# Identity products on TensorE in the prelude of a chunked attention and SwiGLU kernel

## The chip, the cores and the metric

The kernel runs on one core of a Trainium2 chip. The metric is the device time of one execution in microseconds (us); lower is better. The engines are TensorE (PE, with its weight loads as PEld), VectorE (DVE), ScalarE (ACT), GpSimd (POOL) and SyncE (SP), which here only issues transfers.

## The reference

Attention inside chunks of 64 tokens, 8 heads of 64, 8 sequences of 576 tokens, and on its output, as 4608 rows of 512, an RMS norm and a gated feed-forward layer of width 1536:

```python
scores = scale * np.matmul(q_c, k_c.transpose(0, 1, 2, 4, 3))
scores = scores - np.max(scores, axis=-1, keepdims=True)
attn = np.exp(scores)
attn = attn / (np.sum(attn, axis=-1, keepdims=True) + 1e-09)
out = np.matmul(attn, v_c)
...
rms = np.sqrt(np.mean(x * x, axis=-1, keepdims=True) + 1e-06)
xn = x / rms * rms_g
g = xn @ w_gate
silu = g * (1.0 / (1.0 + np.exp(-g)))
val = xn @ w_val
return (silu * val @ w_out).astype(np.float32)
```

q, k, v are float32. The weights arrive as 64-bit numbers and are turned into float32 on the chip.

## The kernel before, in words

The 4608 rows go in nine tiles of 512. The first three ("plain" tiles, t = 0, 1, 2) are computed one by one: for each f of 12 blocks of the hidden width, `gated(f)` makes the gate (12 products of 128x512 into `ps_g`) and the value (12 into `ps_v`), Silu and their product `sg`, and `down(f - 1)` adds 12 products to four accumulators `acc`. The other six tiles go in three pairs through a scheme that saves products. Each operand is split in a high part `h` and a low part `l` of the type fp32r, and three products (h with h, l with h, h with l) stand for one. A product of the gate of f = 3 so needs both parts of its weights. `ps_g` and `ps_v` have one bank each: the gate of f + 1 waits for the Silu of f, the value of f + 1 for VectorE's product `sg` of f.

Attention works on units of 256 tokens, each two halves of 128 (i = 0, 1 are unit 0, i = 2, 3 unit 1). Per half: `scores` (products of 64x64), `softmax` on VectorE and the exponential on ScalarE (`e`), `att_transpose` (4 transposes into `ps_t`, copied by ScalarE to `eT`), `att_values` (into `ps_o`), `first_norm` (VectorE writes `x`). Then the squares are summed on ScalarE (`ss_u`), the root is taken on GpSimd (`ri_u`), ScalarE scales x, `x_turn_unit` transposes it on TensorE (`ps_x`), ScalarE makes `xh` and VectorE `xl`.

The prelude does this for units 0 and 1, and then tile 0 starts. Beside it, and through most of tile 0, the 18 blocks of weights are converted. Each takes a load (`raw`, 1 MB), two steps on ScalarE (the absolute value of the high word to `w`, and the low word scaled in place), three on VectorE (a clamp, a shift, the sign), a cast on ScalarE (high part of `parts`), and a subtraction on VectorE (low part). Blocks 0, 1, 3, 4, 6, 7 and so on hold the gate and value weights of f = 0, 1, 2, 3, 4, 5; the blocks between them hold output weights. Units 2 and 3 are worked on inside tile 0, at f = 0 and f = 5.

Until tile 1 the order of instructions on each engine is set by a scheduler from priorities (the order of the code, raised or lowered by `high_priority`) and its own estimates; each engine then works through its queue in that order. `tc.issue_after(x)` lets instructions of a block stand only behind x on x's engine. SyncE's queue is also in order: a store that waits for VectorE holds the loads behind it.

The prelude's main lines before:

```python
    scores(0, s0)
    scores(1, s1)
    softmax(0)
    softmax(1)
    att_transpose(0)
    softmax_sum(0)
    att_transpose(1)
    softmax_sum(1)
...
    scores(2, s2)
    scores(3, s2)
    softmax_both(1, s2)
```

Of the kernel before, what the change touches and what calls it, by code (L numbers as in the profile page):

```python
# [17 lines left out]
P = 128  # L18
# [62 lines left out]
def tile_chunk_attn_swiglu(  # L81
# [82 lines left out]

    conv = {}

    def conv_load(n):
# [4 lines left out]
    def conv_start(n):  # L172
        if n < len(pairs):
            words = raws[n].bitcast(I32).rearrange("p (n w) -> p n w", w=2)
            low, high = words[:, :, 0], words[:, :, 1]
            w = wp.tile([P, 2 * DM], F32, name="w")
            conv[n] = low, high, w
            nc.scalar.activation(w, high.bitcast(F32), AF.Abs, scale=2.0**16)  # L178
            nc.scalar.mul(low, low.bitcast(U32), LOW_SCALE)

    def conv_join(n):
        if n < len(pairs):


            low, high, w = conv[n]
            wi = w.bitcast(I32)
            nc.vector.tensor_scalar(w, w, HIGH_LEAST, HIGH_MOST, op0=ALU.max, op1=ALU.min)
            nc.vector.scalar_tensor_tensor(
                wi, wi, 3, low, op0=ALU.logical_shift_left, op1=ALU.bitwise_or
            )  # L190
            nc.vector.scalar_tensor_tensor(
                wi, high, -(2**31), wi, op0=ALU.bitwise_and, op1=ALU.bitwise_or
            )
# [10 lines left out]
            nc.scalar.copy(parts[:, 0].rearrange("p i c -> p (i c)"), w)  # L204
            if kind == "up":
                nc.sync.dma_start(wfd[f], w)

    def conv_end(n):
        if 0 <= n < len(pairs):
            w, parts = conv.pop(n)  # L210
            hi, lo = (parts[:, i].rearrange("p i c -> p (i c)") for i in range(2))
            nc.vector.tensor_tensor(lo, w, hi.bitcast(F32), op=ALU.subtract)

# [13 lines left out]

    state = {}

    def load_unit(u):  # L230
# [27 lines left out]
    def scores(i, banks):  # L258
        st, s = state[i], i % 2
        st["s"] = [b[:, s].rearrange("p (a k) -> p a k", k=CH) for b in banks]  # L260
        for pr in range(NPAIR):
            for j in range(2):
                for c in range(2):
                    tok = s * P + c * CH
                    rows = slice(j * D, (j + 1) * D)
                    nc.tensor.matmul(  # L266
                        st["s"][j][c * CH : (c + 1) * CH, pr],
                        st["q"][rows, pr, tok : tok + CH],
                        st["k"][rows, pr, tok : tok + CH],
                        start=True,  # L270
                        stop=True,
                    )

    def softmax(i):
# [8 lines left out]
        nc.scalar.activation(e, e, AF.Exp, scale=SCALE)  # L283

    def softmax_sum(i):
        st = state[i]
        rs = st["rs"] = small.tile([P, NPAIR, 2, 1], F32, name="rs")
        nc.vector.tensor_reduce(rs, st["e"], axis=AX.X, op=ALU.add)
        nc.vector.tensor_scalar_add(rs, rs, 1e-9)
        nc.vector.reciprocal(rs, rs)  # L290

# [26 lines left out]
    def att_transpose(i, pool=None):  # L318
        st = state[i]
        e = st["e"].rearrange("p a j k -> p a (j k)")  # L320
        eT = st["eT"] = att.tile([P, NPAIR, P], F32, tag="eT", name="eT")
        pt = bank(pool or ps_a, "ps_t").rearrange("p (a k) -> p a k", k=P)
        for pr in range(NPAIR):
            nc.tensor.transpose(pt[:, pr], e[:, pr], ident)
        nc.scalar.copy(eT, pt)

# [116 lines left out]
    def att_values(i, banks):  # L443
# [3 lines left out]
        for pr in range(NPAIR):  # L447
            for j in range(2):
                for c in range(2):
                    rows = slice(j * CH, (j + 1) * CH)  # L450
                    nc.tensor.matmul(
                        st["o"][j][c * CH : (c + 1) * CH, pr, :],
# [3 lines left out]
                        stop=True,  # L456
                    )

    def inv_rms(xs, spent):
# [45 lines left out]
    def x_turn_unit(u, d, pool):  # L505
        pt = state["xt", u, d] = bank(pool, "ps_x")
        for k in range(2):
            for s in range(2):
                at = (2 * k + s) * P
                src = x[:, 2 * u + s, (d + k) * P : (d + k + 1) * P]  # L510
                nc.tensor.transpose(pt[:, at : at + P], src, ident)

    def x_high_unit(u, d):
        pt = state["xt", u, d]
        for k in range(2):
            hi = xh[d + k][:, u * UT : (u + 1) * UT]
            nc.scalar.mul(hi, pt[:, k * UT : (k + 1) * UT], g_col[:, d + k : d + k + 1])  # L517

    def x_low_unit(u, d):
        pt = state.pop(("xt", u, d))  # L520
        for k in range(2):
            hi, lo = (part[d + k][:, u * UT : (u + 1) * UT] for part in (xh, xl))
            nc.vector.scalar_tensor_tensor(
                lo,
# [7 lines left out]
    def first_norm(i):  # L532
# [3 lines left out]
        for j in range(2):  # L536
            nc.vector.tensor_tensor(
                xv[:, j],
# [15 lines left out]
    def first_scale(u, shared):  # L554
# [5 lines left out]
        else:  # L560
            nc.scalar.mul(two, two, ri[:, 1:2])

    def softmax_both(u, banks):
# [5 lines left out]
        for j in range(2):  # L569
            by_row = banks[j].rearrange("p s (a k) -> p s a k", k=CH)  # L570
            nc.vector.tensor_reduce(mx[:, j], by_row, axis=AX.X, op=ALU.max)
            for s, (st, e) in enumerate(zip(both, es)):
                nc.vector.tensor_tensor(
                    e[:, :, j], st["s"][j], mx[:, j, s].broadcast_to([P, NPAIR, CH]), op=ALU.subtract
                )
        for e in es:
            nc.scalar.activation(e, e, AF.Exp, scale=SCALE)

# [538 lines left out]
    att_values(0, o)  # L1117
    first_norm(0)
    o = two_banks(ps_acc, "ps_o")
    att_values(1, o)  # L1120
    first_norm(1)
    scores(2, s2)
    scores(3, s2)
    softmax_both(1, s2)
# [6 lines left out]
    softmax_sum(3)  # L1131
    o = two_banks(ps_h, "ps_o")
    att_values(2, o)
# [190 lines left out]
```

## Time and profile before

| | us |
|---|---|
| median of 3 runs | 902.25 |
| lowest and highest | 901.88, 902.53 |
| profiled execution, its own time | 903.82 |
| its span (first to last instruction) | 902.0 |
| TensorE busy in it | 878.8 (97%) |
| mean granted TensorE clock | 0.99 |

How to read the rows. A row of the timeline gives the start in us from the span's start, the length, engine, line, operation, tiles (written <- read), shapes, how many instructions were put together (x32), and in brackets the idle time of the engine just before with what ended it. A row of the waits gives who waited for whom, then the total, how often and the longest. A row of the windows gives the stretch, and for PE, PEld, DVE, ACT and POOL the busy time and instructions, then the granted TensorE clock (1.00 is full), the share of the DMA engines and GB/s. Line numbers are those of the kernel before.

### The profile page before, as it was taken

Reading aid. Unit: us, or ns where it says so; the run is one execution under the profiler, and the core shown is the slowest. Engines: PE = TensorE matmul, PEld = TensorE weight load, DVE = VectorE, ACT = ScalarE, POOL = GpSimd, SP = SyncE. Lnnn points to the kernel's source line nnn. Section 1 sums busy time; section 2 is a strip of 40 time slices with the busy share of each in tenths; the row PEclk is TensorE's granted clock in tenths of the full one; section 3 lists DMA queues with packets and bytes.
Section 4 is the critical chain, followed back from the end, with each engine's and each line's share of the span. In section 5 each row is a group of like instructions: output and inputs, shape, how many; then the busy total and the mean of one; then the engine's idle time right before and its main releaser. Section 6 shows DMA issues by size and latency. Waiting matters only on the chain.

```text
span 902.0 us, 17424 instructions
## 1 busy us (share of the span) xinstructions
PE 878.8 (97%) x6828; PEld 720.7 (80%) x6828; DVE 606.3 (67%) x962; ACT 456.5 (51%) x775; POOL 181.3 (20%) x157
## 2 busy tenths in 40 slices
PE   4899999999999999999999999999999999999998
PEld 3688878888888888888888878888888888888886
DVE  6999865454568755985677987565769963334775
ACT  5997934343545564544545644336547432222452
POOL 0003040234200000233323002333330004323200
PEclk8799999999999999999999999999999999999999
DMA  9699999778977874887897867786866795445442
GB/s 350 271 340 325 323 329 360 244 235 258 301 247 242 236 222 148 317 272 263 269 322 286 303 249 282 244 297 212 303 231 245 277 342 187 156 157 199 180 163 94
DMA packets 85794, 231.84 MB, mean 257 GB/s; under 512 B 8912, under 2 KB 45264, under 8 KB 71504
## 3 DMA queue, kind: packets, MB, share of 16 engines
q1 hardware_dynamic: 84656, 230.20, 72.8%
q8 instruction: 54, 0.88, 0.4%
q10 hardware_dynamic: 1056, 0.52, 0.2%
q14 instruction: 28, 0.23, 0.1%
HBM read 167.25 MB, written 63.44 MB: 256 GB/s over the span
## 4 chain that ended last, share of the span: by engine, by line
PE 85%; ACT 6%; DMA 4%; DVE 3%; issue 1%; SPq 0%; POOL 0%; ACTq 0%; POOLq 0%
PE ps_c L820 11%; PE ps_a L820 11%; PE ps_b L820 11%; PE acc L627 9%; PE ps_g L592 8%; PE ps_v L592 8%; PE ps_d L820 6%; PE ps_c L1032 5%; PE ps_a L1032 5%; PE ps_b L1032 4%; PE ps_d L1032 3%; DMA wr<-wsd 2%; PE ps_o L393 2%; PE ps_s L266 2%; ACT w L178 1%; DMA raw<-w_up_dram 1%
## 5 line engine op out<-in xcount | busy, mean ns | idle before, releaser
L820 PE MATMUL ps_a<-xp,wr 128*128 128x512 f32 x432 | 104.5, 390 | 0.8 <-DMA wr<-wsd 0.7
L820 PE MATMUL ps_c<-xp,wr 128*128 128x512 f32 x432 | 104.6, 391 | 0.5 <-DMA wr<-wsd 0.5
L820 PE MATMUL ps_b<-xp,wr 128*128 128x512 f32 x432 | 104.5, 391 | 0.0
L592 PE MATMUL ps_g<-xh,parts 128*128 128x512 f32 x288 | 96.7, 396 | 0.9 <-ACT xh L517 0.6
L820 PEld LDWEIGHTS ps_a<-xp,wr 128*128 128x128 f32 x432 | 80.9, 188 | 18.5 <-DMA wr<-wsd 1.7
L592 PE MATMUL ps_v<-xh,parts 128*128 128x512 f32 x288 | 95.0, 390 | 0.5 <-DVE sg L614 0.5
L820 PEld LDWEIGHTS ps_c<-xp,wr 128*128 128x128 f32 x432 | 80.6, 188 | 17.6 <-issue 0.6
L820 PEld LDWEIGHTS ps_b<-xp,wr 128*128 128x128 f32 x432 | 80.7, 188 | 17.1
L627 PE MATMUL acc<-parts,gh 128*128 128x512 f32 x288 | 89.9, 394 | 0.0
L908 POOL TENSOR_TENSOR g<-u,u 128x512 f32<-128x512 f32 x18 | 23.2, 1288 | 269.7 <-ACT u L876 161.2
L592 PEld LDWEIGHTS ps_g<-xh,parts 128*128 128x128 f32 x288 | 54.4, 189 | 13.6 <-ACT sg L610 1.0
L592 PEld LDWEIGHTS ps_v<-xh,parts 128*128 128x128 f32 x288 | 54.2, 188 | 12.1 <-DVE sg L614 0.9
L940 ACT CAST gh<-g 128x512 fp32r<-128x512 f32 x72 | 43.6, 622 | 37.3 <-PE ps_b L1032 13.2
L627 PEld LDWEIGHTS acc<-parts,gh 128*128 128x128 f32 x288 | 53.2, 188 | 11.2
L945 DVE TENSOR_TENSOR gl<-g,gh 128x512 fp32r<-128x512 f32 x72 | 50.3, 705 | 15.8 <-PE ps_a L1032 6.6
L898 POOL TENSOR_TENSOR p<-p,p 128x512 f32<-128x512 f32 x36 | 46.7, 1308 | 53.0 <-DVE rs L354 35.9
L592 PE MATMUL ps_g<-xl,parts 128*128 128x512 f32 x144 | 56.5, 392 | 0.0
L627 PE MATMUL acc<-parts,gl 128*128 128x512 f32 x144 | 56.2, 390 | 0.0
L592 PE MATMUL ps_v<-xl,parts 128*128 128x512 f32 x144 | 56.0, 389 | 0.0
L876 ACT ACTIVATE p<-p 128x512 f32<-128x512 f32 x36 | 22.8, 633 | 58.4 <-POOL p L898 52.6
L820 PE MATMUL ps_d<-xp,wr 128*128 128x512 f32 x216 | 52.3, 391 | 0.0
L885 DVE TENSOR_TENSOR u<-ps_b,p 128x512 f32<-128x512 f32 x36 | 24.5, 687 | 40.1 <-PE ps_b L820 36.5
(150 smaller groups left out, 1701.5 us busy)
## 6 DMA issues: line engine op xcount, KB each, us to landing
wr<-wsd SPq DMA_DIRECT2D x63, 1024.0 KB, 6.8
wo<-osd SPq DMA_DIRECT2D x30, 1024.0 KB, 7.8
raw<-w_up_dram SPq DMA_DIRECT2D x12, 1024.0 KB, 10.6
vt<-v_dram SPq DMA_DIRECT2D x18, 512.0 KB, 6.1
wsd<-parts SPq DMA_DIRECT2D x18, 512.0 KB, 8.3
qt<-qT_dram SPq DMA_DIRECT2D x17, 512.0 KB, 5.2
kt<-kT_dram SPq DMA_DIRECT2D x17, 512.0 KB, 5.9
away_e<-e SPq DMA_DIRECT2D x28, 256.0 KB, 3.1
```

Of the source, the lines that this page charges most:

```text
L266: nc.tensor.matmul(st["s"][j][c * CH : (c + 1) * CH, pr], st["q"][rows, pr, tok : tok + CH], st["k"][rows, pr, tok : tok + CH], start=True ...
L393: nc.tensor.matmul(st["o"][(2 * c + t) * Q : (2 * c + t + 1) * Q, h * D : (h + 1) * D], eT[c][rows, t, h], vt[rows, c, h], start=True, sto ...
L592: nc.tensor.matmul(ps, a[f][:, cols], b[dt], start=(dt == 0 and i == 0), stop=(dt == NDT - 1 and i == 2),)
L627: nc.tensor.matmul(acc[s], a[:, cols], b, start=(f == 0 and i == 0), stop=(f == NF - 1 and i == 2),)
L820: nc.tensor.matmul(ps, w[:, a, m, cols], xp[:, b, kt], start=start and kt == 0 and i == 0, stop=stop and kt == 1 and i == 2, skip_group_ch ...
L876: nc.scalar.activation(t, t if src is None else src, AF.Silu)
L885: nc.vector.tensor_tensor(kp["u2"], b["b"], kp["p1"], op=add)
L898: nc.gpsimd.tensor_tensor(kp["p5"], kp["p1"], kp["p5"], op=add)
L908: nc.gpsimd.tensor_tensor(g[:, 0, 1], kp["u2"], kept[0]["u2"], op=mult)
L940: nc.scalar.copy(gh, src)
L945: nc.vector.tensor_tensor(gl, src, pair[0].bitcast(F32), op=ALU.subtract)
L1032: nc.tensor.matmul(banks[m][name], w[:, (0, 1, 0)[k], m * P : (m + 1) * P], (gh, gh, gl)[k], start=opens and i == 0 and k == 0, stop=not ( ...
```

## The change

A helper `keep_busy` is added, which multiplies the first columns of the 128x128 identity by themselves into a bank of PSUM that is not read afterwards, at low priority and behind a given instruction. `whole` products have 128 columns, `half` ones 64. It is called five times in the prelude: 2 + 14 products ahead of the first scores, 1 behind the transposes of half 0, 1 behind those of half 1, 6 + 20 behind the scores of half 3, and 10 + 10 behind the x transposes of unit 0: 64 products. Some steps are tied behind others with `issue_after`, and a table `CONV_BEHIND` of 25 entries ties steps of the first seven weight conversions on ScalarE and VectorE behind named steps of the prelude (the diff shows its first lines). The tile `ps_o` of half 2 is opened earlier in the code. No operation is removed.

```diff
+    CONV_BEHIND = {
+        (0, "abs"): ("exp", 1),
+        (0, "low"): ("eT", 1),
...
+    def behind(n, what):
+
+        held = ExitStack()
+        if (n, what) in CONV_BEHIND:
+            held.enter_context(tc.issue_after(mark[CONV_BEHIND[n, what]].ins))
+        return held
...
-            nc.scalar.activation(w, high.bitcast(F32), AF.Abs, scale=2.0**16)
-            nc.scalar.mul(low, low.bitcast(U32), LOW_SCALE)
+            with behind(n, "abs"):
+                nc.scalar.activation(w, high.bitcast(F32), AF.Abs, scale=2.0**16)
+            with behind(n, "low"):
+                nc.scalar.mul(low, low.bitcast(U32), LOW_SCALE)
...
+    def keep_busy(bank, whole, half, behind):
+
+        with ExitStack() as held:
+            held.enter_context(tc.high_priority(offset=-URGENT))
+            if behind is not None:
+                held.enter_context(tc.issue_after(behind.ins))
+            for cols in [P] * whole + [CH] * half:
+                one = ident[:, :cols]
+                done = nc.tensor.matmul(bank[:cols, 0, :cols], one, one, start=True, stop=True)
+        return done
...
-    scores(0, s0)
-    scores(1, s1)
+    with tc.issue_after(keep_busy(s2[0], 2, 14, None).ins):
+        done = scores(0, s0)
+    with tc.issue_after(done.ins):
+        done = scores(1, s1)
     softmax(0)
     softmax(1)
-    att_transpose(0)
+    with tc.issue_after(done.ins):
+        done = att_transpose(0)
+    keep_busy(s2[0], 1, 0, done)
     softmax_sum(0)
-    att_transpose(1)
-    softmax_sum(1)
+    with tc.issue_after(keep_busy(s2[0], 1, 0, att_transpose(1)).ins):
+        softmax_sum(1)
+        o = two_banks(ps_h, "ps_o")
+        att_values(0, o)
+        first_norm(0)
+        spare = o = two_banks(ps_acc, "ps_o")
+        done = att_values(1, o)
+        first_norm(1)
+    with tc.issue_after(done.ins):
+        scores(2, s2)
     o = two_banks(ps_h, "ps_o")
...
-    scores(3, s2)
+    asked = scores(3, s2)
...
     for d in range(0, NDT, 2):
-        x_turn_unit(0, d, ps_a)
+        first_turned = x_turn_unit(0, d, ps_a)
...
+    keep_busy(spare[0], 6, 20, asked)
+    keep_busy(spare[0], 10, 10, first_turned)
     conv_start(0)
     conv_step(EARLY)
```

What this does to the order shows at four places. In the rows a name is a tile (`ps_x` the x transposes, `xh_119` and `xl_123` the high and low part of x's first quarter), and line numbers after are those of the kernel after.

TensorE, end of the prelude, before:

```order
L451 MATMUL ps_o_397<-vt,eT 64x64 x2
L511 MATMUL ps_x<-ident,x 128x128 x12
L592 MATMUL ps_g<-xh_119,parts 128x512
L592 MATMUL ps_v<-xh_119,parts 128x512
L511 MATMUL ps_x<-ident,x 128x128 x4
L592 MATMUL ps_g<-xl_123,parts 128x512
```

and after:

```order
L568 MATMUL ps_x<-ident,x 128x128 x8
L281 MATMUL ps_o_301<-ident 128x128 x10
L281 MATMUL ps_o_301<-ident 64x64 x10
L568 MATMUL ps_x<-ident,x 128x128 x8
L652 MATMUL ps_g<-xh_119,parts 128x512
L652 MATMUL ps_v<-xh_119,parts 128x512
L652 MATMUL ps_g<-xl_123,parts 128x512
```

The identity products stand between the transposes of unit 0 and unit 1, and all 16 x transposes now stand ahead of the first gate product. Further on the 64 score products of unit 2, which stood behind `down` of f = 0, stand between the value of f = 0 and the gate of f = 1.

ScalarE, from the copies `eT` of unit 1 to the scaling of its x (L549 is a sum of squares, L517 makes `xh`), before:

```order
L325 COPY eT<-ps_t 128x512
L178 ACTIVATE w<-raw 128x1024
L325 COPY eT<-ps_t 128x512
L204 CAST parts<-w 128x1024
L179 ACTIVATE raw<-raw 128x1024
L549 ACTIVATE e,ss_u<-x 128x512 x2
L517 ACTIVATE xh_119<-ps_x,g_col 128x256
L145 ACTIVATE ss_u<-ss_u 128x2
L517 ACTIVATE xh_120<-ps_x,g_col 128x256
L557 ACTIVATE x<-x,ri_u 128x512
```

and after:

```order
L380 COPY eT<-ps_t 128x512 x2
L246 CAST parts<-w 128x1024
L215 ACTIVATE w<-raw 128x1024
L609 ACTIVATE e,ss_u<-x 128x512
L575 ACTIVATE xh_119<-ps_x,g_col 128x256
L575 ACTIVATE xh_120<-ps_x,g_col 128x256
L217 ACTIVATE raw<-raw 128x1024
L609 ACTIVATE e,ss_u<-x 128x512
L575 ACTIVATE xh_121<-ps_x,g_col 128x256
L145 ACTIVATE ss_u<-ss_u 128x2
L575 ACTIVATE xh_122<-ps_x,g_col 128x256
L617 ACTIVATE x<-x,ri_u 128x512
```

Three `xh` rows stand ahead of the sum `ss_u` where one stood.

VectorE, between the subtraction (L212, L255) for block 3 and that for block 4, whose low part f = 3 needs (L614, L674 make `sg`, L619, L679 `gl`). Before:

```order
L614 TENSOR_TENSOR sg<-ps_v,sg 128x512
L187 TENSOR_SCALAR w<-w 128x1024
L188 SCALAR_TENSOR_TENSOR w<-w,raw 128x1024
L619 TENSOR_TENSOR gl<-sg,gh 128x512
L191 SCALAR_TENSOR_TENSOR w<-raw,w 128x1024
L571 TENSOR_REDUCE mx_u<-ps_s_548 128x8
L571 TENSOR_REDUCE mx_u<-ps_s_549 128x8
L573 TENSOR_TENSOR e<-ps_s_548,mx_u 128x4x64 x2
L573 TENSOR_TENSOR e<-ps_s_549,mx_u 128x4x64 x2
L212 TENSOR_TENSOR parts<-w,parts 128x1024
```

and after, from behind the `sg` of f = 1:

```order
L643 TENSOR_REDUCE rs_u<-e 128x8 x2
L228 SCALAR_TENSOR_TENSOR w<-w,raw 128x1024
L679 TENSOR_TENSOR gl<-sg,gh 128x512
L644 TENSOR_SCALAR rs_u<-rs_u 128x16
L232 SCALAR_TENSOR_TENSOR w<-raw,w 128x1024
L645 RECIPROCAL rs_u<-rs_u 128x16
L226 TENSOR_SCALAR w<-w 128x1024 x2
L228 SCALAR_TENSOR_TENSOR w<-w,raw 128x1024 x2
L674 TENSOR_TENSOR sg<-ps_v,sg 128x512
L232 SCALAR_TENSOR_TENSOR w<-raw,w 128x1024
L679 TENSOR_TENSOR gl<-sg,gh 128x512
L255 TENSOR_TENSOR parts<-w,parts 128x1024
```

Block 4's subtraction now stands behind the `sg` and `gl` of f = 2 and a clamp and a shift of block 6, all of which stood behind it.

SyncE, from the second pair of loads on, before:

```order
L206 DMA wfd_128<-w 128x1024
L170 DMA raw<-w_out_dram 128x1024
L206 DMA wfd_129<-w 128x1024
L170 DMA raw<-w_up_dram 128x1024 x2
L234 DMA qt<-qT_dram 128x1024
L206 DMA wfd_130<-w 128x1024
```

and after:

```order
L248 DMA wfd_128<-w 128x1024
L288 DMA qt<-qT_dram 128x1024
L289 DMA kt<-kT_dram 128x1024
L206 DMA raw<-w_out_dram 128x1024
L248 DMA wfd_129<-w 128x1024
L290 DMA vt<-v_dram 128x1024
L288 DMA qt<-qT_dram 128x1024
L710 DMA wsd_140<-parts 128x4x256
L206 DMA raw<-w_up_dram 128x1024
L710 DMA wsd_141<-parts 128x4x256
L206 DMA raw<-w_up_dram 128x1024
L248 DMA wfd_130<-w 128x1024
```

The q, k and v of unit 2, q of unit 3 and two stores of weight parts pass ahead of two weight loads.

More of the change, by code (lines that the diff above doesn't have):

```diff
@@ L165, in tile_chunk_attn_swiglu @@
     conv = {}
+    mark = {}
+    CONV_BEHIND = {
+        (0, "abs"): ("exp", 1),
+        (0, "low"): ("eT", 1),
+        (1, "abs"): ("scale", 0),
+        (1, "low"): ("exp", 3),
+        (2, "abs"): ("eT", 2),
+        (0, "cast"): ("eT", 3),
+        (2, "low"): ("eT", 3),
+        (1, "cast"): ("high", 1, 0),
+        (3, "abs"): ("high", 1, 0),
+        (3, "low"): ("high", 1, 2),
+        (4, "abs"): ("high", 1, 2),
+        (4, "low"): ("high", 1, 2),
+        (5, "low"): ("high", 1, 2),
+        (6, "low"): ("high", 1, 2),
+        (0, "clamp"): ("sum", 1),
+        (0, "shift"): ("norm", 0),
+        (0, "sign"): ("norm", 1),
+        (1, "clamp"): ("less", 3),
+        (1, "shift"): ("sum", 3),
+        (1, "sign"): ("sum", 3),
+        (0, "end"): ("norm", 3),
+        (2, "clamp"): ("norm", 3),
+        (2, "shift"): ("low", 0, 0),
+        (2, "sign"): ("low", 1, 0),
+        (1, "end"): ("low", 1, 0),
+    }
+    def behind(n, what):
[3 more added lines that the diff above has]
+        return held
     def conv_load(n):
@@ L186, in conv_join @@
             wi = w.bitcast(I32)
[L187 to L193, printed above, removed]
+            with behind(n, "clamp"):
+                nc.vector.tensor_scalar(w, w, HIGH_LEAST, HIGH_MOST, op0=ALU.max, op1=ALU.min)
+            with behind(n, "shift"):
+                nc.vector.scalar_tensor_tensor(
+                    wi, wi, 3, low, op0=ALU.logical_shift_left, op1=ALU.bitwise_or
+                )
+            with behind(n, "sign"):
+                nc.vector.scalar_tensor_tensor(
+                    wi, high, -(2**31), wi, op0=ALU.bitwise_and, op1=ALU.bitwise_or
+                )
             parts = wts.tile([P, 2, 2, DM], F32R, tag="wts", name="parts")
@@ L203, in conv_join @@
                 hi[at], lo[at] = parts[:, 0, i], parts[:, 1, i]
-            nc.scalar.copy(parts[:, 0].rearrange("p i c -> p (i c)"), w)
+            with behind(n, "cast"):
+                nc.scalar.copy(parts[:, 0].rearrange("p i c -> p (i c)"), w)
             if kind == "up":
@@ L211, in conv_end @@
             hi, lo = (parts[:, i].rearrange("p i c -> p (i c)") for i in range(2))
-            nc.vector.tensor_tensor(lo, w, hi.bitcast(F32), op=ALU.subtract)
+            with behind(n, "end"):
+                nc.vector.tensor_tensor(lo, w, hi.bitcast(F32), op=ALU.subtract)
     wfd = [dram.tile([P, 2 * DM], F32, name=f"wfd{n}") for n in range(NF)]
@@ L265, in scores @@
                     rows = slice(j * D, (j + 1) * D)
-                    nc.tensor.matmul(
+                    done = nc.tensor.matmul(
                         st["s"][j][c * CH : (c + 1) * CH, pr],
@@ L272, in scores @@
                     )
+        return done
     def softmax(i):
@@ L289, in softmax_sum @@
         nc.vector.tensor_scalar_add(rs, rs, 1e-9)
-        nc.vector.reciprocal(rs, rs)
+        mark["sum", i] = nc.vector.reciprocal(rs, rs)
     def softmax_rows(u, banks):
@@ L323, in att_transpose @@
         for pr in range(NPAIR):
-            nc.tensor.transpose(pt[:, pr], e[:, pr], ident)
-        nc.scalar.copy(eT, pt)
+            done = nc.tensor.transpose(pt[:, pr], e[:, pr], ident)
+        mark["eT", i] = nc.scalar.copy(eT, pt)
+        return done
     def turned_softmax(u, banks):
@@ L450, in att_values @@
                     rows = slice(j * CH, (j + 1) * CH)
-                    nc.tensor.matmul(
+                    done = nc.tensor.matmul(
                         st["o"][j][c * CH : (c + 1) * CH, pr, :],
@@ L457, in att_values @@
                     )
+        return done
     def inv_rms(xs, spent):
@@ L510, in x_turn_unit @@
                 src = x[:, 2 * u + s, (d + k) * P : (d + k + 1) * P]
-                nc.tensor.transpose(pt[:, at : at + P], src, ident)
+                turned = nc.tensor.transpose(pt[:, at : at + P], src, ident)
+        return turned
     def x_high_unit(u, d):
@@ L522, in x_low_unit @@
             hi, lo = (part[d + k][:, u * UT : (u + 1) * UT] for part in (xh, xl))
-            nc.vector.scalar_tensor_tensor(
+            mark["low", u, d] = nc.vector.scalar_tensor_tensor(
                 lo,
@@ L560, in first_scale @@
         else:
-            nc.scalar.mul(two, two, ri[:, 1:2])
+            mark["scale", u] = nc.scalar.mul(two, two, ri[:, 1:2])
     def softmax_both(u, banks):
@@ L572, in softmax_both @@
             for s, (st, e) in enumerate(zip(both, es)):
-                nc.vector.tensor_tensor(
+                mark["less", 2 * u + s] = nc.vector.tensor_tensor(
                     e[:, :, j], st["s"][j], mx[:, j, s].broadcast_to([P, NPAIR, CH]), op=ALU.subtract
                 )
-        for e in es:
-            nc.scalar.activation(e, e, AF.Exp, scale=SCALE)
+        for s, e in enumerate(es):
+            mark["exp", 2 * u + s] = nc.scalar.activation(e, e, AF.Exp, scale=SCALE)
     def softmax_whole(u, banks):
```

15 lines of the change are left out of this document (5 added, 10 removed).

## The prediction

> **What bounds the kernel now.** I read the page's first part, then TensorE's waits, then the windows of the first 40 us, and last the rows of each engine there.
>
> ```profile
> span 902.0 us, 17424 instructions
> PE 878.8 (97%) x6828; PEld 720.7 (80%) x6828; DVE 606.3 (67%) x962; ACT 456.5 (51%) x775; POOL 181.3 (20%) x157
> PE ps_s L266 <- DMA x<-qT_dram: 6.4, 2, 5.1
> PE ps_t L324 <- ACT e L577: 5.6, 1, 5.6
> PE ps_x L511 <- ACT x L557: 2.2, 1, 2.2
> PE ps_v L592 <- DVE sg L614: 0.5, 1, 0.5
> PE ps_g L592 <- ACT sg L610: 0.4, 1, 0.4
> 5.00:10.00 5.00, 3.31 (x68) 2.66 (x68) 2.72 (x8) 0.63 (x1) 0.00 (x0) 1.00 1.04 379
> 15.00:20.00 5.00, 0.35 (x24) 0.21 (x16) 4.71 (x10) 2.99 (x7) 0.71 (x1) 0.78 1.02 419
> 20.00:25.00 5.00, 3.64 (x60) 3.05 (x64) 4.59 (x10) 5.00 (x8) 0.00 (x0) 0.50 1.01 419
> 35.00:40.00 5.00, 4.63 (x21) 3.53 (x20) 4.83 (x8) 4.97 (x6) 0.00 (x0) 1.00 0.07 25
> ```
>
> TensorE is busy 878.8 of 902.0 us; nearly all of its rest lies in the prelude. Behind it the time is the moment at which the dense stream of products begins, plus what later waits add. In a row of the windows the columns are PE, PEld, DVE, ACT and POOL busy, then the granted clock: 0.78 in 15 to 20, 0.50 in 20 to 25, full again in 35 to 40. Not only TensorE matters here: VectorE is busy 4.6 to 4.8 of 5 us in these windows, ScalarE up to all of them.
>
> ```profile
> 5.11 1.13 PE L266 MATMUL ps_s<-x 64*64 64x64 f32 x32 [5.11 <-DMA x<-qT_dram]
> 7.54 1.13 PE L266 MATMUL ps_s<-x 64*64 64x64 f32 x32 [1.30 <-DMA x<-qT_dram]
> 12.34 1.98 PE L451 MATMUL ps_o<-vt,eT 64*64 64x64 f32 x64 [0.39 <-ACT eT L325]
> 14.10 1.25 PE L266 MATMUL ps_s<-kt,qt 64*64 64x64 f32 x64
> 20.91 1.97 PE L324 MATMUL ps_t<-ident,e 128*128 128x128 f32 x8 [5.57 <-ACT e L577]
> 25.52 1.97 PE L511 MATMUL ps_x<-ident,x 128*128 128x128 f32 x8
> 29.66 1.52 PE L511 MATMUL ps_x<-ident,x 128*128 128x128 f32 x4 [2.17 <-ACT x L557]
> 31.74 0.80 PE L592 MATMUL ps_g<-xh,parts 128*128 128x512 f32 x1 [0.57 <-ACT xh L517]
> 39.76 0.50 PE L592 MATMUL ps_g<-xh,parts 128*128 128x512 f32 x1 [0.37 <-ACT sg L610]
> 40.32 0.62 PE L592 MATMUL ps_g<-xh,parts 128*128 128x512 f32 x2
> 55.27 1.03 PE L324 MATMUL ps_t<-ident,e 128*128 128x128 f32 x8
> 58.42 0.39 PE L592 MATMUL ps_g<-xh,parts 128*128 128x512 f32 x1
> 65.05 0.73 PE L627 MATMUL acc<-parts,gh 128*128 128x512 f32 x2
> 102.76 0.39 PE L592 MATMUL ps_g<-xh,parts 128*128 128x512 f32 x1
> ```
>
> Eight transposes take 1.97 us at 20.91 and at 25.52, and 1.03 at 55.27. Thirty-two products of scores take 1.13 us at 5.11 and 7.54, while 64 take 1.25 at 14.10. So the prelude runs at half speed except around 14 to 18 us, though the granted column reads 1.00 in 5 to 10. Half speed ends near 35.
>
> [...]
>
> **The change, part by part.** A plain f32 product is two instructions: one call of `scores` issues 4 x 2 x 2 = 16, and each of the first two shows 32 in its row; a transpose is one. A product of 128 columns therefore costs between one and two of the transpose rows. I take two: 0.44 us at half speed, 0.22 at full (half of that for 64 columns).
>
> - *16 ahead of the first scores:* 2 x 0.44 + 14 x 0.22 = 4.0 us at half speed, from about 1.3 us when the identity is made, so to 5.3. The scores start at 5.11 before: up to 0.2 late, hidden by the 1.30 us wait ahead of 7.54. If the gate opens in this stretch, the second scores end 0.5 us sooner (1.13 to about 0.6).
> - *One behind each of the first two transposes:* 0.2 to 0.4 us, inside the 0.39 wait at 12.34.
> - *26 behind the scores of the second unit:* 6 x 0.22 + 20 x 0.11 = 3.5 us at full speed, 7.0 at half, in a rest of 5.57. The clock is full when they begin, so hidden.
> - *20 between the two sets of x transposes:* 10 x 0.22 + 10 x 0.11 = 3.3 us, 6.6 at half, in a rest of 2.17 that grows to about 4 when the transposes before it take half the time. Hidden at full speed, not at half.
>
> What this buys depends on the other two engines.
>
> ```profile
> 13.51 0.76 DVE L537 TENSOR_TENSOR x<-ps_o,rs 128x256 f32<-128x256 f32 x2 [0.97 <-PE ps_o L451]
> 21.28 1.14 ACT L179 ACTIVATE raw<-raw 128x1024 int32<-128x1024 uint32 x1
> 27.87 0.20 ACT L145 ACTIVATE ss_u<-ss_u 128x2 f32<-128x2 f32 x1
> 28.88 0.72 ACT L557 ACTIVATE x<-x,ri_u 128x512 f32<-128x512 f32 x1 [0.45 <-POOL ri_u L146]
> 39.74 0.69 DVE L614 TENSOR_TENSOR sg<-ps_v,sg 128x512 f32<-128x512 f32 x1
> 50.13 1.28 DVE L571 TENSOR_REDUCE mx_u<-ps_s 128x8 f32<-128x512 f32 x2
> 51.33 1.41 DVE L573 TENSOR_TENSOR e<-ps_s,mx_u 128x256 f32<-128x256 f32 x4
> 52.65 1.22 DVE L212 TENSOR_TENSOR parts<-w,parts 128x1024 fp32r<-128x1024 f32 x1
> 53.79 0.69 DVE L187 TENSOR_SCALAR w<-w 128x1024 f32<-128x1024 f32 x1
> 56.12 1.27 DVE L583 TENSOR_REDUCE rs_u<-e 128x8 f32<-128x512 f32 x2
> 57.31 1.21 DVE L188 SCALAR_TENSOR_TENSOR w<-w,raw 128x1024 int32<-128x1024 int32 x1
> 58.44 0.68 DVE L619 TENSOR_TENSOR gl<-sg,gh 128x512 fp32r<-128x512 f32 x1
> 98.67 1.11 ACT L204 CAST parts<-w 128x1024 fp32r<-128x1024 f32 x1
> 99.81 1.23 DVE L212 TENSOR_TENSOR parts<-w,parts 128x1024 fp32r<-128x1024 f32 x1 [0.47 <-ACT parts L204]
> 123.01 0.68 DVE L614 TENSOR_TENSOR sg<-ps_v,sg 128x512 f32<-128x512 f32 x1
> ```
>
> 1. *First half of the prelude.* Scores and value products at full speed end the first wait of VectorE (13.51) about 1.0 us sooner; the low half of the first weight block, due on ScalarE, lets 0.8 of it through. ScalarE's row at 21.28 moves to 20.45.
> 2. *ScalarE's new order.* From there ScalarE runs without a rest to the sum at 27.87, 6.59 us. The order now has two more `xh` scalings ahead of that sum (0.36 each, their start-to-start), so it falls at 20.45 + 7.31 = 27.76. The gain of step 1 is spent: unit 1's x is scaled 0.1 us sooner, no more.
> 3. *The gate and value products of f = 0.* Eight transposes at full speed end near 30.95 and the first product starts there, not at 31.74. All 24 products run at 0.23 us each (from 40.32 two take 0.62, of which one is 0.39), 5.5 us, to about 36.45 and in plain order; the scores of the third unit (1.1 us, moved ahead of the second gate) give ScalarE time for its table and Silu (36.8). Before, those products ended by 39.39 (the 0.37 wait ends at 39.76), so with the wait TensorE is 3.3 us ahead.
> 4. *VectorE takes part of it back.* Its product of 39.74 can start at 36.85, behind ScalarE's Silu. From there to the low part of the weights for f = 3 stand, in the new order and by start-to-start in these rows, two subtractions for weights (1.14 each), three steps of the third unit's softmax (1.20, 1.32, 1.19), six shifts and signs (1.13), three clamps (0.60), six gate steps (0.60) and two small ones: 18.5 us, and about 0.5 of waits for ScalarE, so 55.9, done at 57.1. TensorE reaches the gate of f = 3 (58.42 before) at 54.75, has 0.95 us of work that needs no low part, and waits 1.4. The row of 65.05 comes at 57.1 + 20 x 0.23 + 1.05 = 62.7: 2.35 ahead.
> 5. *f = 8.* ScalarE has two more table loads ahead of it (1.29 each); its cast (98.67) then ends near 100.4 and the subtraction (99.81) at 101.6, while TensorE, 2.4 ahead of 102.76, wants it at 101.0: 0.6 lost. A transposed tile comes 0.3 late behind it.
> 6. *f = 10.* VectorE has 3.4 us less ahead of the row of 123.01 in the new order: TensorE's 0.5 us wait goes.
>
> Sum: 2.35 - 0.6 - 0.3 + 0.46 = 1.9 us faster. SyncE's queue moves too: q, k and v of the third unit and two stores of 0.5 MB each pass ahead of two weight loads, 2.5 MB or 6.0 us at the 419 GB/s of these windows; by my times those blocks (landing near 40 and 44) are first used at 46 and 49, so it costs nothing while 5 us are left. From tile 1 on nothing else moves that a wait of TensorE names.
>
> The profiled execution took 903.82 us over its span of 902.0, the runs have a median of 902.25: the sum makes the span 900.1 and the median 900.35.
>
> **The rivals.**
>
> *The gate stays half shut early* (first scores to value products as slow as now). Step 1 gives nothing, step 2 makes the sum 0.7 late, the first product starts near 31.75 as before, VectorE follows 0.8 later, and step 4 leaves 1.55 instead of 2.35: 1.1 in all, 901.2. For it: before, the clock opened only at about 14. Against: sixteen plain products without a rest are as long a burst as any there.
>
> *The gate closes again before the dense stream.* Between the last filler (about 27.3) and 30.95 stand 3.6 us of rest and transposes alone; before, the clock fell about 2.6 us after the scores of 14.10 ended. Products then run at half speed for about 3.4 us, the time the stream needed before (31.74 to 35): 1.7 us later at step 3, but step 4's wait of 1.4 shrinks by as much, and 0.4 of the gain is lost: 900.75. [...]
>
> *VectorE does not hold TensorE back:* step 4's rows prove shorter, TensorE keeps 3.3 and the wait of step 6 goes: 898.5. Against it, VectorE's almost full windows.
>
> *Slower: the last fillers run at half speed.* They stand in TensorE's queue ahead of unit 1's transposes. From 26 us, 6.6 us at half speed end at 32.6 instead of 29.66, 2.9 late, plus the late ScalarE sum; if VectorE's new order then also starves f = 3, nothing of steps 3 to 6 is left and 2.0 us are lost: 904.2. It decides when the fillers outlast the rest by more than the 2.5 us that plain order and full speed give afterwards. Against it, the fillers open the gate themselves.
>
> *It does nothing:* the weight conversion on VectorE sets the pace and order and fillers cancel: 902.2.
>
> **Chances.** Forecast 0.42 (899.4 to 901.0), early gate shut 0.20, gate closing again 0.12, no hold by VectorE 0.09, nothing 0.07, slower 0.10. A difference of 0.2%, 1.8 us, is about what a measurement of this kernel can tell. Faster than 900.45: six tenths of the forecast, all of the third rival, a third of the second and a little of the first, 0.42. Slower than 904.05: 0.10 with stray cases. Within: 0.48. The unknown cost of a product (one or two transposes) moves the fillers only inside their rests. The range, 898.7 to 902.6, leaves out the slower rival and half of the 898.5 case.
>
> **What would show it.** Right: the granted clock at 1.00 through 15 to 35 and eight transposes in about 1 us; the wait for `e` shrunk to a rest filled by the identity rows; the second root at the same 28 us; a wait of TensorE of 1 to 2 us near 56 for VectorE's `parts`, and none for the gate product near 121. Wrong: first gate product later than 31.7, clock 0.50 beside the fillers, waits for weight loads near 45, or no wait near 56.

## The result and the profile after

The changed kernel is slower: 909.84 us (median of 4 runs, 906.46 to 910.19) against 902.07, ratio 1.0082 [1.0062, 1.0103]. In a second session with 12 runs it took 906.68 (904.17 to 910.82) against 902.92, ratio 1.0038 [1.0018, 1.0058]. Brackets are 95% intervals. The two intervals do not meet although the kernel is the same, so ratios of different sessions that lie less than some 0.4% apart decide nothing by themselves. The profiled run is the shortest of the first four, 906.46 us with a span of 904.7. Line numbers below are those of each kernel.

The page's first lines after the change, then TensorE's waits (total, how often, longest), then windows cut where the granted clock changes (columns as before):

```profile
span 904.7 us, 17695 instructions
PE 888.9 (98%) x6956; PEld 731.1 (81%) x6956; DVE 606.3 (67%) x962; ACT 460.0 (51%) x777; POOL 189.6 (21%) x157
```

```profile
PE ps_s L320 <- issue: 2.6, 1, 2.6
PE ps_x L568 <- ACT x L617: 2.1, 1, 2.1
PE ps_t L379 <- ACT e L338: 1.8, 2, 1.3
PE ps_t L379 <- ACT e L361: 1.2, 1, 1.2
PE ps_g L652 <- DVE parts L255: 0.4, 1, 0.4
```

```profile
16.70:23.40 6.70, 6.16 (x53) 5.81 (x53) 5.43 (x14) 4.53 (x6) 0.30 (x1) 0.50 1.00 417
23.50:33.60 10.10, 7.80 (x138) 7.17 (x136) 6.99 (x13) 7.72 (x16) 1.02 (x1) 1.00 1.01 405
33.70:37.10 3.40, 3.19 (x11) 2.35 (x11) 1.52 (x4) 2.40 (x6) 0.00 (x0) 0.50 1.18 369
```

TensorE is 10.1 us busier, its rests in the prelude are smaller, yet the span is 2.7 us longer (and the shortest of four). A wait stands there that before did not have: 2.6 us with no releaser ("issue": the profile shows nothing that ended it). The clock is at half from 16.7 to 23.4 and from 33.7 to 37.1, and at full for the 10.1 us between: two, one and three times some 3.4 us. TensorE's rows:

```profile
5.68 0.99 PE L320 MATMUL ps_s<-x 64*64 64x64 f32 x32
13.75 0.93 PE L320 MATMUL ps_s<-kt,qt 64*64 64x64 f32 x48 [0.89 <-DMA kt<-kT_dram]
17.24 0.70 PE L320 MATMUL ps_s<-kt,qt 64*64 64x64 f32 x16 [2.56 <-issue]
17.88 6.62 PE L281 MATMUL ps_o<-ident 128*128 128x128 f32 x52
24.42 1.09 PE L379 MATMUL ps_t<-ident,e 128*128 128x128 f32 x8
27.80 3.71 PE L281 MATMUL ps_o<-ident 128*128 128x128 f32 x40
35.64 0.80 PE L652 MATMUL ps_g<-xh,parts 128*128 128x512 f32 x1
68.04 0.73 PE L687 MATMUL acc<-parts,gh 128*128 128x512 f32 x2
105.53 0.66 PE L379 MATMUL ps_t<-ident,e 128*128 128x128 f32 x4 [1.16 <-ACT e L361]
```

The scores of the second unit stop after 48 of 64 rows; the last 16 come 2.56 us later. The clock falls to half in that rest, so the 26 identity products (52 rows) take 6.62 us instead of the 3.5 of my estimate, and the transposes behind them start at 24.42, not at 20.91. The first gate product comes at 35.64 (31.74 before), the row of 65.05 at 68.04. Between there and the start of tile 1 another 1.5 us are lost (table below); the wait at 105.53 is the largest in that stretch. From tile 1 to the end this run takes 758.2 us and before 760.0 (1.0 of the difference in waits for loads), so what it loses it has lost by tile 1.

The same products in the traces of all kernels, in us. "More" is the number of TensorE's instructions beyond the 13,847 that the trace of before holds, waits on semaphores included. The columns after it are the first gate product, the row of 65.05 (`down` of f = 1), the first gate product of tile 1, the span, and the waits without a releaser of over 0.5 us from 140 us on. A median is of all runs of its session, a ratio goes to the runs of before in the same session.

| kernel | more | gate | `down` | tile 1 | span | late waits | median, ratio to before |
|---|---|---|---|---|---|---|---|
| before | 0 | 31.74 | 65.05 | 141.98 | 902.0 | none | |
| after | 257 | 35.64 | 68.04 | 146.51 | 904.7 | none | 909.84, 1.0082 [1.0062, 1.0103] |
| e0, again | 257 | 33.78 | 66.84 | 147.81 | 909.0 | 2.0 | 906.68, 1.0038 [1.0018, 1.0058] |
| e2, no products | 0 | 31.09 | 64.43 | 141.74 | 899.5 | none | 902.49, 0.9996 [0.9979, 1.0014] |
| e1, 256 columns | 93 | 31.50 | 64.29 | 144.92 | 907.0 | 3.6 | 911.46, 1.0096 [1.0062, 1.0129] |
| e4, e1 + 11 small | 137 | 32.24 | 65.65 | 146.28 | 908.3 | 3.1 | 909.35, 1.0071 [1.0043, 1.0099] |
| f1, after + tie | 256 | 33.77 | 65.97 | 143.34 | 901.0 | none | 904.16, 1.0022 [1.0003, 1.0041] |
| f2, e1 + tie | 92 | 31.84 | 64.14 | 141.46 | 906.4 | 4.5 | 908.32, 1.0058 [1.0035, 1.0080] |
| g1, before + 23 small | 92 | 30.80 | 64.11 | 140.85 | 908.6 | 5.5 | 913.01, 1.0104 [1.0076, 1.0132] |
| g2, before + 64 small | 256 | 31.64 | 65.51 | 141.87 | 909.4 | 2.5 | 907.09, 1.0057 [1.0030, 1.0084] |
| h2, 512 columns, two ties | 52 | 31.47 | 62.63 | 140.32 | 907.8 | 5.2 | 910.62, 1.0089 [1.0066, 1.0112] |
| h3, 8 of 512, two ties | 32 | 32.27 | 63.94 | 142.27 | 903.7 | 1.1 | 905.21, 1.0026 [1.0012, 1.0041] |
| i1, as h2, count 256 | 256 | 32.14 | 63.78 | 142.31 | 900.0 | none | 903.17, 1.0019 [1.0005, 1.0033] |
| j1, as i1, no ties | 257 | 32.59 | 65.00 | 144.59 | 903.2 | none | 906.69, 1.0035 [1.0018, 1.0051] |

### The profile page after: what moved, and what is told of

Read it like the earlier page. It is cut to its first block, busy times and chain, and to the rows that moved or that the text cites. A ratio compares the mean times of both kernels' runs of the same rounds, so it can differ in the third digit from the quotient of the medians.

```text
span 904.7 us, 17695 instructions
## 1 busy us (share of the span) xinstructions
PE 888.9 (98%) x6956; PEld 731.1 (81%) x6956; DVE 606.3 (67%) x962; ACT 460.0 (51%) x777; POOL 189.6 (21%) x157
## 4 chain that ended last, share of the span: by engine, by line
PE 88%; DVE 4%; DMA 3%; ACT 3%; issue 1%; SPq 0%; DVEq 0%; ACTq 0%
PE ps_c L880 11%; PE ps_b L880 11%; PE ps_a L880 11%; PE acc L687 9%; PE ps_g L652 9%; PE ps_v L652 8%; PE ps_d L880 5%; PE ps_c L1092 5%; PE ps_a L1092 5%; PE ps_b L1092 4%; PE ps_d L1092 3%; PE ps_o L449 2%; PE ps_s L320 2%; DMA wr<-wsd 1%; DMA kt<-kT_dram 1%; DVE w L228 1%
```

## The experiments

The runs led to theory T: three separate losses, a wait for instructions that makes the prelude late, exponentials that a new order splits at f = 7, and later waits for instructions whose places go with the count of TensorE's instructions (theory B is this third part).

**e0: the same kernel again.**

> The changed kernel again, for a second profile. All theories: 906 to 910 us. Theory F (TensorE runs out of fetched instructions): a rest with no releaser of 2 to 3 us stands in the scores of the fourth half (three quarters of them done, about 449 instructions of TensorE from its start), the clock falls to half behind it, and the 26 identity products behind the scores take over 6 us. If the clock gate decides on a grid of its own (3.4 us steps), the places where the clock changes lie elsewhere in this profile, and the time may differ by up to 3.4 us from 906.5.

As theory F said: a 2.53 us wait after 48 of the 64 rows, and 5.39 us for the 26 products. The clock changes at other places and the prelude ends 1.9 us sooner than in the first profile; but here the wait near 105 (2.06 us) brings the clock to half as well, and a second wait without a releaser, 2.0 us, stands at 488. Windows of this run:

```profile
102.00:105.60 3.60, 1.54 (x9) 0.98 (x8) 1.40 (x3) 3.56 (x9) 0.00 (x0) 1.00 1.20 328
105.70:109.10 3.40, 3.40 (x10) 2.69 (x9) 3.18 (x4) 3.40 (x5) 0.00 (x0) 0.50 0.82 249
```

**e2: the order without the products.** All calls of `keep_busy` are left out, the ties stay. Rival O says that the new order of steps costs the time, rival D that any product ahead of the transposes in TensorE's queue makes them late, whatever the count.

```diff
-    with tc.issue_after(keep_busy(s2[0], 2, 14, None).ins):
-        done = scores(0, s0)
+    done = scores(0, s0)
...
-    keep_busy(spare[0], 6, 20, asked)
-    keep_busy(spare[0], 10, 10, first_turned)
```

> No identity products at all, the ties of order (the table of conversions and the rest) kept; the scheduler resorts some steps of tile 0. Theory F: no rest in the scores, prelude at half speed as before the change, 900 to 903. Rival O: 905 to 910. Rival D: 900 to 903.

Ratio 0.9996 [0.9979, 1.0014]: the ties and the table of conversions cost and bring nothing that can be measured. The loss needs the products. (Without them the scheduler also puts tile 0 in another order, so this does not show that every order of the changed kernel is free.)

**e1 and e4: fewer instructions of the same width, and the count restored.**

```diff
-            for cols in [P] * whole + [CH] * half:
-                one = ident[:, :cols]
-                done = nc.tensor.matmul(bank[:cols, 0, :cols], one, one, start=True, stop=True)
+            left = P * whole + CH * half
+            while left:
+                n = min(2, left // P)
+                many = ident.rearrange("p (o k) -> p o k", o=1).broadcast_to([P, n, P])
+                out = bank[:, 0].rearrange("p (a k) -> p a k", k=P)[:, :n]
+                done = nc.tensor.matmul(out, ident, many, start=True, stop=True)
+                left -= n * P
```

> Same columns of identity products in the same places, but as products of 256 columns: 21 products instead of 62 in the three groups (44, 72 and 48 instructions fewer). Theory F: no rest inside the scores of the fourth half, the clock stays full there, the 26's stand-in ends by 20.5 and the transposes of the second unit start near 20.4 instead of 24.4; time 900 to 903. Rival O (the new order of steps costs the time): 905 to 910. Rival D (any filler in TensorE's queue ahead of the transposes makes them late, whatever its count of instructions): 905 to 909, transposes near 24.

> The kernel with 256-column products, and 11 products of 16 columns ahead of the first group: as many instructions as in the changed kernel up to the scores of the fourth half (44 more than with wide ones alone), hardly any time, and the same order on every engine. Theory F: the rest of 2 to 3 us in those scores is back at the same instruction (after 48 of 64 rows), time 2 to 6 us above the wide kernel. Rivals O and D: no such rest, the same time as the wide kernel within 0.5.

TensorE's rows in e1:

```profile
13.45 1.16 PE L324 MATMUL ps_s<-kt,qt 64*64 64x64 f32 x64 [0.65 <-DMA kt<-kT_dram]
17.12 2.32 PE L284 MATMUL ps_o<-ident 128*128 128x256 f32 x10 [0.82 <-issue]
19.96 1.18 PE L383 MATMUL ps_t<-ident,e 128*128 128x128 f32 x8 [0.53 <-ACT e L641]
```

In e1 the prelude does what F said: no rest in the scores, a shorter one (0.82 us) in the products behind them, transposes at 19.96, first gate product at 31.50 and 0.76 us ahead in the `down` row. So identity products ahead of the transposes need not make them late, against rival D. The time was a miss for every theory: 911.46. Of it 3.7 us are lost between `down` and tile 1, and 3.6 in waits without a releaser at 427, 613 and 639 us. In e4 the wait in the scores did not come back: a miss too. The first packet on the instruction queue, which in the changed kernel began at 14.9 us, ahead of the end of the wait, began at 10.7 here. So in these two traces the wait went with the moment of that packet, and not with the count alone; what sets that moment is open. The late waits were there again (1.4, 0.7 and 1.0 us). Counted from TensorE's first instruction, those of e1 stand behind numbers 7617, 10689 and 11201, those of e4 behind 6081, 7617 and 10689: all lie a multiple of 256 behind the 449 of the changed kernel. Its page counts 55 packets on that queue (q8) for TensorE's 14,104 instructions, the page of before 54 for 13,847, so 256 to a packet. These are the pieces of 256 in the texts below. These two runs gave the two theories that follow.

**f1 and f2: the exponentials of unit 3 held together.**

```diff
-        with urgent():
+        with ExitStack() as held:
+            held.enter_context(urgent())
+            if f == 7 and "rows" in mark:
+                held.enter_context(tc.issue_after(mark.pop("rows").ins))
             nc.scalar.activation(sg, pg, AF.Silu)
```

(`mark["rows"]` is the last exponential of `softmax_rows`.) ScalarE's rows in the changed kernel, where the last two of 16 exponentials stand behind the Silu of f = 7 with a table load on each side, and then in f1:

```profile
100.56 0.38 ACT L361 ACTIVATE e<-ps_s,mx_u 128x64 f32<-128x64 f32 x1
101.05 1.28 ACT L670 ACT_TABLE_LOAD   x1
102.35 0.60 ACT L670 ACTIVATE sg<-ps_g 128x512 f32<-128x512 f32 x1
102.96 1.28 ACT L361 ACT_TABLE_LOAD   x1
104.26 0.31 ACT L361 ACTIVATE e<-ps_s,mx_u 128x64 f32<-128x64 f32 x1
105.07 0.31 ACT L361 ACTIVATE e<-ps_s,mx_u 128x64 f32<-128x64 f32 x1
```

```profile
100.54 0.39 ACT L361 ACTIVATE e<-ps_s,mx_u 128x64 f32<-128x64 f32 x1
101.04 1.28 ACT L673 ACT_TABLE_LOAD   x1
102.33 0.60 ACT L673 ACTIVATE sg<-ps_g 128x512 f32<-128x512 f32 x1
```

> The changed kernel with one more tie: the Silu of f = 7 in tile 0 stands behind the last exponential of unit 3 on ScalarE, as it did before the change, so two table loads fewer lie between that unit's exponentials. Theory T (three separate losses: a late prelude, the split exponentials at f = 8, and waits for instructions): TensorE's wait for e near 105 us (1.2 to 2.1) goes, and so does the loss of 1.5 to 4 us between 100 and 106; 903 to 905 us, 2 to 4 below the changed kernel. Rival P (the prelude alone sets the loss, the wait near 105 is slack that is given back later): within 0.7 of the changed kernel, 906 to 909.

> The kernel with 256-column products and the same tie. Theory T: TensorE is 1 to 1.5 us ahead of before at 58 us and still 0.5 to 1.5 ahead at 125; what is left is waits without a releaser (for instructions), 1 to 4 us in all; 902 to 908 us, 3 to 4 below the 911.5 of the wide kernel. Rival P: the same as the wide kernel within 1.

The transposes of unit 3 need the last exponential: 105.4 in the one, 100.9 in the other. TensorE's wait falls from 1.2 (2.3 in e1) to 0.2 us. From `down` to tile 1 the changed kernel loses 1.5 us (4.0 in e0), f1 only 0.4; e1 loses 3.7, f2 0.4. What f1 holds at tile 1 it keeps: from there to the end it takes 757.7 us, the changed kernel 758.2. This is as theory T said, and by the traces rival P falls. The times lean the same way, f1 1.0022 to e0's 1.0038 and f2 1.0058 to e1's 1.0096, but the intervals overlap.

**g1 and g2: the count alone.** In the kernel before, small products are put into tile 1, and on no other engine does an instruction move in g1 (in g2 two neighbouring rows change places on ScalarE, and two on VectorE).

```diff
+            if t == 1 and f == 1:
+                for _ in range(23):   # 64 in g2
+                    nc.tensor.matmul(acc[0][:32, :16], ident[:, :32], ident[:, :16], start=True, stop=True)
```

> The kernel before, with 23 products of 16 columns (92 instructions, about 1.4 us) in tile 1 ahead of the first product of down: no other instruction is moved on any engine. The pieces of 256 in which TensorE's instructions arrive then end 92 instructions earlier in the work, nearly where they end in the wide kernel (93). Theory B (a piece that ends inside a burst of small products makes TensorE wait): waits of 0.7 to 2 us without a releaser in scores or values, where before had none, 1 to 4 us in all; 904.5 to 907.5. Rival N (those waits are noise of the single run): 903.5 to 904.5, no such waits.

> The same with 64 products (256 instructions, about 3.8 us): the pieces end where they ended in the kernel before. Theory B: no waits for instructions beyond those of before, 905.5 to 906.5, which is only the 3.8 us of the products. Rival N: the same time. The profile decides between them: with theory B, g1 shows such waits and g2 none.

The traces put the products themselves at 1.5 us in g1 and 4.2 in g2 (the rows around them against before). g2's median is 4.6 us above before's, hardly more than its products, though three of its seven runs are 7 to 10 us above it. g1 has 10.5 us more, of which 9 are not its products: that is beyond what theory B expected. TensorE's waits in g1 from 140 us on, and the windows behind the longest:

```profile
PE ps_b L820 <- issue: 3.0, 1, 3.0
PE ps_s L266 <- issue: 1.9, 2, 1.0
PE acc L627 <- issue: 0.7, 1, 0.7
```

```profile
638.50:641.80 3.30, 3.08 (x7) 2.49 (x8) 0.69 (x1) 0.57 (x1) 0.00 (x0) 0.50 0.37 156
641.90:645.00 3.10, 3.10 (x15) 2.42 (x13) 1.84 (x2) 0.60 (x1) 0.00 (x0) 1.00 0.02 5
```

The wait of 3.0 us is followed by 3.3 us at half clock (638.5 to 641.8), in the dense stream, where before had neither. One part of B was wrong: g2's profile has a wait of 2.5 us at 488, where e0 has one, so those places can wait in some runs even with the count of before.

**h2, h3 and i1: a version with everything mended, at three counts.** Products of 512 columns (2 and one of 128 ahead of the scores, the two single ones, 4, and 3 and one of 384), the tie of f1, and a tie on VectorE:

```diff
+        (6, "clamp"): ("end", 4),
+        (6, "shift"): ("end", 4),
```

h3 has only 2, 3 and 3 products of 512 and no single ones. i1 is h2 with 30 and 29 products of 64 columns as second and third group:

```diff
-    keep_busy(spare[0], 6, 20, asked)
-    keep_busy(spare[0], 10, 10, first_turned)
+    keep_busy(spare[0], 0, 30, asked)
+    keep_busy(spare[0], 0, 29, first_turned)
```

> Identity products of 512 columns (11 in the three groups and one of 128 and one of 384 columns beside the two single ones: some 53 instructions more than the kernel before instead of 257), the tie of the Silu of f = 7, and a second tie on VectorE: clamp and shift of block 6 stand behind the subtraction of block 4, whose low part f = 3 needs. Theory T with B: the wait for parts at f = 3 goes (1 us), TensorE is 1.5 to 2.5 ahead of before at 65 us; of the waits for instructions one near 610 us is left, since the pieces end 53 instructions earlier than in the kernel before; 900 to 903 us. Rival S (late waits come with any identity product, whatever the count): 906 to 909 as the 256-column kernel with its tie.

> The same with 8 products of 512 columns in all (2, 3 and 3), 32 instructions more than the kernel before. Theory B: no wait for instructions from 140 us on in the profile, other than those that before shows in some runs; 899.5 to 902 us if the clock still stays full in the prelude, 901 to 903 if a group of three is too short for that. Rival S: 906 to 909.

> The kernel with products of 512 columns and both ties, except that the second and third group are made of 30 and 29 products of 64 columns, as in the changed kernel: 256 instructions more than the kernel before, so that the pieces of 256 end where they ended before; the order on the other four engines is the same to the row. Theory B: none of the four waits for instructions that lie between 300 and 615 us there; the lead of the prelude (1.5 to 2.4 us at 58 us, 1 to 1.7 at 125) reaches the end, 899.5 to 902.5 us, 8 to 10 below the kernel with 53 instructions more. A wait for instructions inside the second group (before 17.5 us) is expected, since instruction 449 falls there, and costs nothing while the group ends by 20.3. Rival S (late waits come with any identity product): 907 to 911.

h2's early part came out as told: TensorE at 62.63 in the `down` row, 2.4 ahead, and 1.7 ahead at tile 1. Its end did not: 910.62, with four late waits where I expected one. i1 stands in the same order as h2 on the four other engines, and takes 7.5 us less by the medians of their two sessions, 1.0019 against 1.0089 by the ratios, whose intervals lie far apart. TensorE's waits without a releaser from 140 us on in h2; in i1 there are none, only these two for loads:

```profile
PE acc L696 <- issue: 2.1, 1, 2.1
PE ps_c L889 <- issue: 1.5, 1, 1.5
PE ps_g L658 <- issue: 0.9, 1, 0.9
PE ps_s L326 <- issue: 0.6, 1, 0.6
```

```profile
PE ps_a L890 <- DMA wr<-wsd: 0.3, 1, 0.3
PE ps_c L890 <- DMA wr<-wsd: 0.3, 1, 0.3
```

Theory B holds in its main point, rival S falls. Over all 14 traces: of the eight whose count is that of before or 256 or 257 more, six have no such wait and two (e0 and g2) have one, at the same instruction; the six with 32 to 137 more have one to four. h3 was a miss: 905.21 us where I expected 899.5 to 903, with a wait of 1.1 us at 320 that theory B did not allow. My time for i1 (899.5 to 902.5) was too low as well: no version here beats the kernel before. In i1 the lead at 58 us is 1.3, not 1.5 to 2.4: its wait of 1.87 us in the second group makes that group end at 20.7, and the transposes stand right behind it. By tile 1 it is 0.3 behind: 2.1 us are lost between the gates of f = 6 and f = 9, 0.8 of them in a wait for a Silu. The clock is at half for 3.4 us twice in its prelude. Why it does not gain more is not settled.

**j1: the prelude alone mended**, i1 without the two ties.

> The changed kernel, without the two ties of the later kernels, and nearly its order: only the shapes of the identity products differ (the first group two of 512 columns and one of 128, the second 30 and the third 29 of 64), so that instruction 449 falls behind the scores of the fourth half and the total is the same 256 more than before. Theory T: the first gate product comes 0 to 0.6 late instead of 2.0 to 3.9, TensorE is 1 to 2 ahead at 58, loses 3 to 4.5 between 100 and 106 for the split exponentials and ends 1.5 to 3 behind before: 904 to 906, some 1 to 3 below the changed kernel. Rival P (the late prelude is the whole loss): 900.5 to 902.5. Rival Q (the split exponentials are the whole loss, a late prelude is made up for by 58 us as VectorE is what holds tile 0): as the changed kernel, 906 to 909.

TensorE's rows in j1: the wait now stands behind the scores, and the transposes start 3.3 us sooner than in the first profile of the changed kernel.

```profile
13.44 1.16 PE L325 MATMUL ps_s<-kt,qt 64*64 64x64 f32 x64
18.11 3.08 PE L286 MATMUL ps_o<-ident 128*64 128x64 f32 x50 [2.26 <-issue]
21.12 1.09 PE L384 MATMUL ps_t<-ident,e 128*128 128x128 f32 x8
65.00 0.73 PE L693 MATMUL acc<-parts,gh 128*128 128x512 f32 x2
103.66 0.66 PE L384 MATMUL ps_t<-ident,e 128*128 128x128 f32 x4 [2.30 <-ACT e L366]
```

The lead is there at 58 us (1.2) and at `down` it is spent (the next wait, 0.57 us, is for VectorE's `parts` at f = 3); then the split exponentials take 2.7 us up to tile 1, more than in the first profile (1.5), because TensorE arrives sooner and waits longer. By times j1 cannot be told from the changed kernel (1.0035 against 1.0038), as rival Q said, and 906.69 lies above theory T's range; the rows (1.2 ahead at 58, then the loss at the split) are those of T. The two losses overlap: mending the prelude alone brought nothing that the times show.

## Why the prediction was wrong

*The step that failed* is the costing of the 26 products: "The clock is full when they begin, so hidden". The price was near (3.5 us at full speed, 7.0 at half; 6.62 measured, most of it with the clock at half; the 20 products took 3.71 at full speed where I had 3.3), and so was the rest to hide it in (in h2 the transposes wait for `e` until 19.95), but the clock was no longer full. Two signs that I had named for being wrong came: a first gate product later than 31.7 and the clock at 0.50 beside the identity products. I took TensorE's instructions to be there whenever they are due. A product is four of them, as each of its two rows has a weight load (for 64 products the page counts 128 more of PE and 128 more of PEld); so the first group and the two single products put 72 ahead, and after the 449th TensorE stands still. Counts of PE and PEld up to 16 us, before and then after:

```profile
0.00:16.00 16.00, 7.44 (x200) 6.25 (x200) 7.65 (x21) 6.33 (x9) 0.72 (x7) 1.00 0.88 322
```

```profile
0.00:16.00 16.00, 9.88 (x220) 8.68 (x221) 8.63 (x21) 7.09 (x12) 0.73 (x7) 1.00 0.88 321
```

441 instructions and 8 that only synchronise (7 waits on semaphores and a DRAIN) make 449; before, TensorE had come only to 409 when it went into its long rest, and the packet of the instruction queue that began at 16.07 us came in it.

*Step 1* (gate open early, that is, the clock at full speed sooner): right; VectorE's first wait ended at 12.41, 1.1 us sooner. The first scores came 0.57 late, where I had said up to 0.2. *Step 2* (the sum at 27.76): 31.41 in the changed kernel, but 27.62 in h2, where the first wait is mended: the working was right, its start was not. *Step 3* (first product 30.95, 3.3 ahead): 35.64; 31.47 and 31.50 in h2 and e1. Even h2 is only 2.3 ahead at f = 2. *Step 4* (the `down` row at 62.7 with a wait of 1.4 us for the low part): 68.04 with a wait of 0.4 at 62; h2, which also takes that wait away, has 62.63. That it meets my 62.7 is luck: a smaller lead without the wait, where I had a larger lead and the wait. *Step 5* is a second term that failed: I counted two table loads and 0.9 us; between `down` and the gate of f = 9, 2.3 us are lost in the changed kernel and 3.4 in j1, and only 1.2 in f1, where the exponentials are not split around the Silu. I had read the loads as a delay of the cast for f = 8 and not asked which instruction of TensorE needs the last exponential. *Step 6* (0.46 back near 123): 0.75. *From tile 1 on nothing moves*: wrong in kind. In the order nothing moved, but the later waits for instructions move with the count. The trace of the changed kernel has none of them; its 257 more is by chance one of the counts at which six of eight traces have none. The first profile holds only 2.7 us of a median loss of 7.8 (3.8 in the second session). e0's, 7.0 longer than before's, is 5.8 behind at tile 1 and has the 2.0 at 488: the same two steps, dearer, and a late wait. How the runs without a profile divide their loss stays open.

*Rivals.* The slower case (0.10) had the mechanism of products at half speed in TensorE's queue ahead of transposes, but at the last group and through the gate, not through missing instructions. Waits for instructions were in none. I had looked for the sign of the gate in a pause of 3.6 us; pauses of 2.06 us (e0) and 2.56 us (the changed kernel) were followed by a clock at half. That the gate would count the transposes in those 3.6 us as rest was my estimate, from TensorE busy 3.64 of 5 us at a clock of 0.50 in 20 to 25 before; no run tests it.

## What to carry to other kernels

Filling work for an idle TensorE was not free here, though by its price every product fitted a rest: with 72 more instructions ahead of them, TensorE stood still for 2.56 us in a burst of small products, and the clock was at half for 6.7 us on top. Few, wide products took the wait out of the scores (e1, h2), but the later waits went with the count, and the fastest version with identity products (i1) has more and narrower ones than h2. So judge any edit of TensorE's stream at two or three counts of instructions before believing its time. Where a scheduler sets the order, ask after each added instruction what it splits: a table switch ahead of the last two of 16 exponentials cost 1.1 to 3.6 us (the changed kernel, e0 and e1 against f1 and f2, from `down` to tile 1), where the best prelude was 2.4 ahead.

## What the runs showed of the hardware

*Instructions.* In the 14 traces there are 28 waits of TensorE over 0.5 us without a releaser. Counted from its first instruction, waits on semaphores included, each stands behind one whose number leaves 193 when divided by 256: 449, 4545, 5057, 5569, 6081, 7617, 8129, 8897, 9921, 10689, 11201. From 14.5 to 17.3 us of the changed kernel, around the first wait, the transfers show one packet on the instruction queue (packets, MB, share), and the page counts 55 of them with 0.90 MB in the whole run, 16 KB each:

```profile
q8 instruction: 1, 0.02, 2.5%
```

```profile
q8 instruction: 55, 0.90, 0.4%
```

That packet begins at 14.86 and ends at 15.96; TensorE goes on at 17.24. If the packets of this queue are taken in order as the pieces of 256, then in 27 of the 28 waits the restart came 2.2 to 2.8 us after the begin of the piece's packet (3.35 in the other, e4 at 343 us), and nowhere in the 14 traces does a piece start less than 2.2 us after its packet begins (2.38 us at the least in the changed kernel, 3.04 in before). The packet begins between 0 and some 300 instructions ahead of its piece; what decides that is open. In these 28 waits the 256 instructions ahead had passed in 1.7 to 7.2 us.

*The clock.* In the windows it changes after some 3.4 us or a multiple of it (6.7, 10.1 and 3.4 in the changed kernel, 3.4 in e0 and 3.3 in g1). A pause of 2.06 us of TensorE at 105 us brought one such stretch at half speed in e0, while one of 2.30 at the same place left it full in j1 (granted clock 1.00 from 33.8 us on; a product at 104.39, behind the pause, takes 0.39 us). So a pause shorter than one such stretch was enough in the one and not in the other. That the moments of change stand on a grid of their own, as the text of e0 weighs, was not shown; a pause that falls well in one run and badly in the next may be a part of why single runs of one kernel in one session lie up to 8 us apart (e1); no run here tests it.
